# Normalized rows turned by a transposing DMA instead of TensorE: three tiles of each block's output and the third and fourth block of x

## The chip, the cores and the metric

The kernel runs on one core of a Trainium2 chip. The metric is the device time of one execution in microseconds (us). Three runs of the kernel before gave 1598.45, 1598.69 and 1598.71 us; the median is 1598.69. A core has five engines that run beside each other, each with its own queue of instructions in order: TensorE (PE; its weight loads are shown as PEld), VectorE (DVE), ScalarE (ACT), GpSimd (POOL) and SyncE (SP), which only issues transfers (DMAs) here. An instruction that waits for another engine or for a DMA holds everything behind it on its own queue.

## The reference

One transformer block on x of 2048 tokens by 512, in float32: attention of 32 heads of 16, and an MLP of width 1792, each behind a layer norm and with a residual.

```python
x = A_x
h = x + _A_ref(_layernorm(x, axis=-1), A_wqkv, A_wo)
h2 = h + _B_ref(_layernorm(h, axis=-1), B_w1, B_w2)
# _A_ref: qkv = x @ wqkv; p = softmax(q k^T * Dh**-0.5); (p v) @ wo
# _B_ref: silu(x @ w1) @ w2
```

## The kernel before

A matmul here contracts over the partitions, so normalized rows (128 tokens on the partitions, 512 features along each) have to be turned into columns (features on the partitions) before they meet a weight. For precision every operand is a pair of float16 numbers, a high part and the rest, and a product is three matmuls: high by high, rest by high, high by rest (`product`, L134). A turned tile is therefore two results: `turn` (L225) does four TensorE transposes of 128x128 with an identity (`tr`, L100, shown as L101 in the profile) into one PSUM bank, ACT copies the bank into the high part in float16 (`act`, L112), and DVE subtracts that from the bank for the rest (`low`, L123; recorded by `dve` at L115 or `pool` at L105).

Tokens go in four blocks of 512, each of four tiles of 128. The places around the change are two.

*The stage of x* (about 20 to 92 us of the span). For each block `b` the loop at L738 runs six units: two of `project_qk` (`("qk", 1)` for K, then `("qk", 0)` for Q, the columns of the first eight heads) and four of `project_v`, one for each tile. While it does so for block `b` it prepares block `b + 1`: statistics and norms (`other_ln` says in which unit), and `turn_x(b + 1, t)` (L789) for the four tiles, in units 1 to 4. Each project_qk stores its result to DRAM (`kd`, `qd`; two stores each, issued on SP), and after the second one the parts of `kd` that the first score maxima need come back, eight loads `ks<-kd` on SP (`load_k`, L778). Between and inside the units stand bursts of score maxima (`burst`, `two_max`, `maximum`): PE writes a pair of PSUM banks, DVE reduces them (`mx`, L294). In this stage blocks 1 and 2 have four PSUM banks for that, so two pairs (`lay_out(sm=range(4), ...)`, L732). ACT also issues loads of raw weights (`dma_beside`, L118) and squares them for norms.

*The output of a block* (three times, first at about 446 to 476 us). In the middle of the following block's attention, one step of the attention loop after the other, `output(b, n)` (L1172) projects tile `n` with `wo`, adds the residual, normalizes tile `n - 1` and turns it: tile 0 in step 2, tile 1 in step 3, tile 2 in step 4 and tile 3 in step 5, into `hth` and `htl`, the columns of the MLP. Right after the last of these steps `finish_block` does the values that are still due and `mlp(b)`, whose first matmul reads all four tiles. The fourth block ends in `finish_last`, with its own order of the same work.

The order on each engine is the order in which the Python code calls it (`keep_in_program_order`); nothing moves an instruction past another on its engine. A DMA also waits for the one that used its completion counter before (there are eight, given out in turn). Buffers come from pools: a tile of a pool with `bufs=2` can be written for the third time only when the readers of the first are done.

Of the kernel before, what the change touches and what calls it, by code (L numbers as in the profile page):

```python
# [10 lines left out]
F32 = mybir.dt.float32  # L11
F32R = mybir.dt.float32r
F16 = mybir.dt.float16
# [7 lines left out]
P = 128  # L21
S = 2048
D = 512
# [3 lines left out]
DC = D // P  # L27
FC = F // P
NB = S // 512
# [61 lines left out]
def attention_mlp_kernel(ctx: ExitStack, tc: tile.TileContext, x, wqkv, wo, w1, w2, out):  # L91
    nc = tc.nc
# [15 lines left out]
    def pin(ins):  # L108
        tc.keep_in_program_order(ins)

    def act(fn, *a, **k):
        pin(getattr(nc.scalar, fn)(*a, **k))  # L112
# [6 lines left out]

    def dma(*a):  # L120
        pin(nc.sync.dma_start(*a))  # L121

    def low(dst, src, high, engine="dve"):  # L123

        if high.dtype == F32R:
            high = high.bitcast(F32)
        (pool if engine == "pool" else dve)("tensor_tensor", dst, src, high, ALU.subtract)
# [22 lines left out]
    def lay_out(**rings):  # L150

        for kind, ring in rings.items():
            banks[kind] = list(ring)
# [315 lines left out]
    with ExitStack() as pa:  # L469
        pb = pa.enter_context(ExitStack())  # L470
        lay_out(sm=range(5), st=range(5, 8))
        wp = pa.enter_context(tc.tile_pool(name="wp", bufs=1))
        wvp = pb.enter_context(tc.tile_pool(name="wvp", bufs=1, side="right"))
        xp = pa.enter_context(tc.tile_pool(name="xp", bufs=3))
# [1 line left out]
        wqk_l = wp.tile([P, DC, 2 * D], F16, name="wqk_l")  # L476
        wv_h = wp.tile([P, DC, D], F16, name="wv_h")
        wv_l = wp.tile([P, DC, D], F16, name="wv_l")
        xth = [wp.tile([P, DC, 512], F16, name=f"xth{b}") for b in range(NB)]
        xtl = [wp.tile([P, DC, 512], F16, name=f"xtl{b}") for b in range(NB)]  # L480

        wqk0_h, wqk0_l = (wvp.tile([P, DC, 2 * P], F32R, name=name) for name in ("wqk0_h", "wqk0_l"))
        wv0_h, wv0_l, xth0, xtl0 = (wvp.tile([P, DC, 512], F32R, name=name) for name in ("wv0_h", "wv0_l", "xt0_h", "xt0_l"))
# [1 line left out]
        xts = [ks[2 + b % 2].rearrange("p a n -> p (a n)").bitcast(F32).rearrange("p (t d) -> p t d", d=D)  # L485
               for b in range(NB)]
# [6 lines left out]
        def load_x(b, parts=1):  # L493
            n = 4 // parts
            for t in range(0, 4, n):
                r0 = b * 512 + t * P
                dma(xts[b][:, t:t + n, :], x[r0:r0 + n * P, :].rearrange("(t p) d -> p t d", p=P))
# [11 lines left out]
        def square_rest(u):  # L509

            n = u - 7
            if 0 <= n < len(pieces):
                square_into(staged[n % 2], staged[n % 2], n)
            n = u - 5
            if 0 <= n < len(pieces):
                dma_beside(staged[n % 2], pieces[n])
# [107 lines left out]
        def project_v(b, t):  # L624
# [3 lines left out]
                  {k: (lambda n=n: burst(n)) for k, n in BESIDE_V1.get((b, t), {}).items()})  # L628
            act("mul", va[:, 4 * b + t, :, 0:DH], ps.rearrange("p (h d) -> p h d", d=DH), v_f)

        def turn_x(b, t):

            turn(xts[b][:, t, :], xth[b][:, :, t * P:(t + 1) * P], xtl[b][:, :, t * P:(t + 1) * P],
                 "sm" if b == 1 else "st")
# [10 lines left out]
        def columns(t):  # L645
            return slice(t * P, (t + 1) * P)
# [83 lines left out]
        for b in range(NB):  # L730
            if b == 1:
                lay_out(sm=range(4), st=(7, 4, 5, 6))  # L732
            if b == NB - 1:
                lay_out(sm=range(6), st=[n for n in banks["st"] if n > 5])
            units = [("qk", 1), ("qk", 0)]
            vs = [("v", t) for t in range(4)]
            found = {}
            for n, (kind, k) in enumerate(units + vs if b else units):  # L738
                tick()
                square_rest(2 + 6 * (b - 1) + n if b else n)  # L740
                rows, (stats, norm, turns) = None, ((), (), ())
                if b + 1 < NB:
                    rows = xts[b + 1]
                    stats, norm, turns = (other_ln if b else first_ln)[n]
                    if b == 2 and n < 4:
                        stats, norm = (((0, 1), (0,)), ((), (1,)), ((3,), (2,)), ((), ()))[n]

                def layer_norm():
                    for of_norm in (kind == "v", kind != "v"):
                        for t in norm if of_norm else stats:  # L750
                            if of_norm:
                                normalize(rows[:, t, :], rows[:, t, :], *found.pop(t), engine="pool" if kind == "v" and (b, n) != (1, 2) else "dve")
                            else:
                                found[t] = statistics(rows[:, t, :], LN)

                if kind == "v":
                    project_v(b, k)
                else:

                    if (b, n) == (0, 1):  # L760
                        load_x(3)
                        for c in range(2):
                            pool("tensor_scalar", scaled[1 - c], raw_v[:, 2 + c], v_w, 1.0, op0=ALU.mult, op1=ALU.mult)
                        split_qk(splits.pop((b, n)))
                    layer_norm()
                    if (b, n) == (1, 0):
                        split_values(0)
                    project_qk(b, k, scale=b > 0)
                    if (b, n) == (0, 1):
                        split_values(1)  # L770
                    if (b, n) in splits:
                        split_qk(splits.pop((b, n)))
                    if k == 0:
                        for i in range(2):
                            for h in range(4):
                                if b == 0:
                                    load_q(i, h)
                                load_k(i, h, b * 512, 512)  # L778
                if b:

                    burst(BESIDE_V[b - 1][kind == "v"][n - 2 if kind == "v" else n])
                if (b, n) == (2, 0):
                    stats, norm = (2,), ()
                if kind == "v" or (b, n) == (2, 0):
                    layer_norm()
                if (b, n) == (2, 2):
                    normalize(rows[:, 3, :], rows[:, 3, :], *found.pop(3), engine="pool")
                for t in turns:
                    turn_x(b + 1, t)  # L789
                if b == NB - 1 and n < DC:  # L790
                    split_x0(n)
                if (b, n) in splits:
                    split_qk(splits.pop((b, n)), "pool")
                if b == 2 and n in (3, 5):
                    fixed_rows(n // 4)
# [23 lines left out]
        for g in range(1, NG // 2):  # L819
            for m, (b, key) in enumerate([(b, 1) for b in range(NB)] + [(b, 0) for b in range(NB)]):  # L820
# [3 lines left out]
                n = 8 * g + m - 12  # L824
# [16 lines left out]
    cpool = ctx.enter_context(tc.tile_pool(name="cpool", bufs=1, side="right"))  # L841
    bp = ctx.enter_context(tc.tile_pool(name="bp", bufs=PTS - EARLY))
    pools.append(bp)
    gp = ctx.enter_context(tc.tile_pool(name="gp", bufs=2))
# [1 line left out]
    ot = [cpool.tile([P, 4, DC, P], F32, name=f"ot{i}") for i in range(2)]  # L846
    wo_h = cpool.tile([P, DC, D], F16, name="wo_h")
    wo_l = cpool.tile([P, DC, D], F16, name="wo_l")
    hth = cpool.tile([P, DC, 512], F16, name="hth")
    htl = cpool.tile([P, DC, 512], F16, name="htl")  # L850
    def values(g):
        i, c = divmod(g, KC)
        n = KC if i < LAST else HALF
# [118 lines left out]
    ws, hx, os = {}, {}, {}  # L972
# [8 lines left out]
    def parts_of(w):  # L981
        return w.bitcast(F16).rearrange("p (s n) -> p s n", s=2)
# [54 lines left out]
    def rows_of(b, t):  # L1037
        return ot[b % 2][:, t].rearrange("p c n -> p (c n)")

    def add_rows(b, t, ps):  # L1040

        dve("scalar_tensor_tensor", rows_of(b, t), ps, wo_f, hx[t], op0=ALU.mult, op1=ALU.add)

    def turn_rows(t):
        turn(hx.pop(t), hth[:, :, t * P:(t + 1) * P], htl[:, :, t * P:(t + 1) * P])

# [125 lines left out]
    def output(b, n):  # L1172

        if n < 4:
            ps = bank()
            weave(project_rows(n, ps), {6: lambda: singles(3)} if n < MORE[b] else {})
            add_rows(b, n, ps)
        if n == 4:

            turn_rows(n - 2)  # L1180
        if 0 < n < 5:
            normalize(hx[n - 1], rows_of(b, n - 1), *found.pop(n - 1))

        if n in (2, 3, 5):
            turn_rows(n - 2)
        if n < 4:
            found[n] = statistics(rows_of(b, n), LN)
# [144 lines left out]
    for g in range(groups):  # L1332
        tick()
        i, c = divmod(g, KC)
# [38 lines left out]
        n = maxima(g)  # L1373
# [61 lines left out]
```

## Time and profile before

| | |
|---|---|
| median of three runs | 1598.69 us |
| the profiled execution | 1598.55 us |
| its span, first to last instruction | 1596.7 us |
| PE busy | 1585.3 us (99%) |
| DVE busy | 1389.7 us (87%) |
| ACT busy | 1207.2 us (76%) |
| POOL busy | 472.6 us (30%) |
| bytes moved | 137.15 MB, mean 86 GB/s |

The profile is one execution. Each row of its timeline has the start and the length in us, the engine and line, the operation, the tile written and the tiles read, the shape and, behind an x, how many like ones were merged; a bracket names idle time of the engine just before and what ended it. Lines named for most rows are those of the recording helpers (L98 for every matmul, L112 for ACT, L115 for DVE, L105 for POOL, L121 for SP), so tiles tell the rows apart. "SPq" rows are transfers being issued by SP: their length is that of the issue, not of the transfer. A matmul's length is its way through the array (about 380 ns); those that follow each other start every 0.216 us, and that pitch is what they cost.

### The profile page before, as it was taken

Reading aid. Unit: us, or ns where it says so; the run is one execution under the profiler, and the core shown is the slowest. Engines: PE = TensorE matmul, PEld = TensorE weight load, DVE = VectorE, ACT = ScalarE, POOL = GpSimd, SP = SyncE. Lnnn points to the kernel's source line nnn. Section 1 sums busy time; section 2 is a strip of 40 time slices with the busy share of each in tenths; the row PEclk is TensorE's granted clock in tenths of the full one; section 3 lists DMA queues with packets and bytes.
Section 4 is the critical chain, followed back from the end, with each engine's and each line's share of the span. In section 5 each row is a group of like instructions: output and inputs, shape, how many; then the busy total and the mean of one; then the engine's idle time right before and its main releaser. Section 6 shows DMA issues by size and latency. Waiting matters only on the chain.

```text
span 1596.7 us, 28487 instructions
## 1 busy us (share of the span) xinstructions
PE 1585.3 (99%) x10524; PEld 477.6 (30%) x10524; DVE 1389.7 (87%) x2054; ACT 1207.2 (76%) x2384; POOL 472.6 (30%) x755
## 2 busy tenths in 40 slices
PE   9999999999999999999999999999999999999999
PEld 6434222222233322222233322222233322222254
DVE  7999999999989889999989889999987889998432
ACT  5545799999964179999963179999974189999732
POOL 5643544544426101211135101211126101211200
PEclk9999999999999999999999999999999999999999
DMA  6667533452423511121223521112133511100232
GB/s 213 173 178 221 134 86 96 107 127 81 116 67 101 156 49 35 39 54 39 50 76 100 152 53 33 39 43 51 49 77 107 159 39 37 34 12 22 74 86 73
DMA packets 111427, 137.15 MB, mean 86 GB/s; under 512 B 29136, under 2 KB 66064, under 8 KB 111288
## 3 DMA queue, kind: packets, MB, share of 16 engines
q1 hardware_dynamic: 104980, 125.17, 29.1%
q10 hardware_dynamic: 6308, 10.17, 2.3%
q8 instruction: 82, 1.34, 0.4%
q14 instruction: 57, 0.47, 0.1%
HBM read 104.68 MB, written 24.85 MB: 81 GB/s over the span
## 4 chain that ended last, share of the span: by engine, by line
PE 71%; ACT 22%; DVE 4%; DMA 1%; issue 1%; POOL 1%; SPq 0%; POOLq 0%; ACTq 0%
PE ps L98 70%; ACT pt L112 22%; DVE mx L294 2%; DVE mx L296 1%; PE ps L101 1%; DMA va<-in_A_wqkv_dram 0%; DMA ks<-in_A_x_dram 0%; DVE st L115 0%; DVE htl L115 0%; DVE hx L115 0%; SPq L121 0%; POOL rs L105 0%; POOL wv_l L105 0%; DVE xtl L115 0%; DVE ot L115 0%
## 5 line engine op out<-in xcount | busy, mean ns | idle before, releaser
L112 ACT ACTIVATE pt<-ps 128x512 f32<-128x512 f32 x2048 | 1009.4, 640 | 147.6 <-PE ps L98 145.8
L296 DVE TENSOR_REDUCE mx<-ps 128x1 f32<-128x512 f32 x1470 | 924.4, 683 | 52.3 <-PE ps L98 23.7
L98 PE MATMUL ps<-pt,va 128*17 128x512 f32 x4096 | 537.5, 598 | 0.3
L98 PE MATMUL ps<-qs,ks 64*128 64x512 f16 x2048 | 532.1, 379 | 2.3 <-DVE htl L115 0.7
L98 PE MATMUL ps<-ks,qs 48*128 48x512 f16 x2048 | 493.7, 380 | 1.5 <-DVE mx L294 1.0
L294 DVE TENSOR_REDUCE mx<-ps 128x2 f32<-128x1024 f32 x289 | 334.9, 1217 | 41.9 <-PE ps L98 40.6
L98 PEld LDWEIGHTS <-ks 64*128 64x128 f16 x2048 | 149.3, 95 | 546.0 <-issue 429.3
L105 POOL TENSOR_TENSOR ri<-rc,minus 128x16 f32<-128x16 f32 x31 | 90.7, 2925 | 235.8 <-DMA rc<-dn 169.9
L98 PE MATMUL ps<-w,gh 128*128 128x512 f16 (+1 forms) x678 | 154.4, 378 | 0.0
L98 PEld LDWEIGHTS <-qs 48*128 48x128 f16 x2048 | 126.2, 94 | 75.1 <-issue 58.3
L98 PEld LDWEIGHTS ps<-pt,va 128*17 128x17 f32 x4096 | 68.8, 95 | 223.9 <-issue 205.4
L98 PE MATMUL ps<-hth,w 128*128 128x512 f16 (+1 forms) x472 | 132.9, 369 | 0.0
L112 ACT ACTIVATE g<-ps,factors 128x512 f32<-128x512 f32 x56 | 38.5, 688 | 123.5 <-PE ps L98 95.4
L105 POOL TENSOR_TENSOR mx<-mx 128x32 f32<-128x32 f32 x52 | 12.5, 240 | 391.2 <-DVE mx L296 384.6
L98 PEld LDWEIGHTS <-w 128*128 128x128 f16 x708 | 66.3, 98 | 80.1 <-issue 12.4
L98 PEld LDWEIGHTS <-gh 128*128 128x128 f16 x678 | 63.1, 98 | 83.0 <-issue 13.7
L98 PE MATMUL ps<-htl,w 128*128 128x512 f16 (+1 forms) x236 | 84.0, 368 | 0.0
L112 ACT ACTIVATE ks<-ps 128x512 f32<-128x512 f32 x30 | 18.0, 599 | 50.3 <-PE ps L98 43.3
L115 DVE SCALAR_TENSOR_TENSOR gh<-g,factors,gh 128x512 f16<-128x512 f32 x14 | 10.5, 751 | 52.2 <-ACT gh L112 52.2
L105 POOL TENSOR_TENSOR sl<-ks,sh 128x512 f16<-128x512 f32 x30 | 34.7, 1156 | 51.5 <-ACT sh L112 34.2
L105 POOL TENSOR_TENSOR gh<-g,gh 128x512 f16<-128x512 f32 x42 | 48.5, 1155 | 3.5
L105 POOL TENSOR_TENSOR ot<-ot,den 128x512 f32<-128x512 f32 (+1 forms) x16 | 20.4, 1274 | 89.9 <-DMA den<-dr 85.5
(155 smaller groups left out, 973.8 us busy)
## 6 DMA issues: line engine op xcount, KB each, us to landing
w<-w2d SPq DMA_DIRECT2D x98, 256.0 KB
ks<-kd SPq DMA_DIRECT2D x120, 192.0 KB
w<-w1d SPq DMA_DIRECT2D x56, 256.0 KB
ks<-in_B_w_dram ACTq DMA_DIRECT2D x28, 256.0 KB
w<-in_B_w_dram SPq DMA_DIRECT2D x28, 256.0 KB
qs<-qd SPq DMA_DIRECT2D x128, 48.0 KB
kd<-sh SPq DMA_DIRECT2D x16, 256.0 KB
qd<-sh SPq DMA_DIRECT2D x16, 256.0 KB
```

Of the source, the lines that this page charges most:

```text
L98: tc.keep_in_program_order(nc.tensor.matmul(*a, **k))
L101: tc.keep_in_program_order(nc.tensor.transpose(*a))
L105: tc.keep_in_program_order(getattr(nc.gpsimd, op)(*a, **k))
L112: pin(getattr(nc.scalar, fn)(*a, **k))
L115: pin(getattr(nc.vector, fn)(*a, **k))
L294: pin(nc.vector.tensor_reduce(of, space[:, n:n + 2, :], axis=AX.X, op=ALU.max))
L296: pin(nc.vector.tensor_reduce(of[:, j:j + 1], space[:, n, :], axis=AX.X, op=ALU.max))
```

## The change

`turn_beside` is a transposing DMA on SP's queue: it takes a tile that holds, for 128 tokens, the high parts of 512 features and then the rests (128 by 1024 in float16, 256 KB) and writes it turned, as eight pieces of 128x128, into the columns of the tile pair.

For x, blocks 2 and 3 (the third and fourth; `if b:`) are no longer turned by PE. `split_x` makes high part and rest in token order out of the normalized rows, on ACT and DVE, into `xh`, a tile of a pool with two buffers; it stands ahead of the unit's projection. The DMA that turns it stands where `turn_x` stood. Block 1 is turned as before. For the output, tiles 0, 1 and 2 of the three blocks that `output` serves are split right after their norm, the high part on ACT and the rest on POOL, and turned by a DMA one step later; tile 3 is turned by PE as before. `xth` and `xtl` of a block, and `hth` and `htl`, become halves of one tile each, so that one DMA can write both.

```diff
+    def turn_beside(dst, cols, src):
+
+        pin(nc.sync.dma_start(dst.rearrange("p s c n -> p (s c) n")[:, :, cols],
+                              src.rearrange("p s d -> p (s d)"), transpose=True))
...
-        xth = [wp.tile([P, DC, 512], F16, name=f"xth{b}") for b in range(NB)]
-        xtl = [wp.tile([P, DC, 512], F16, name=f"xtl{b}") for b in range(NB)]
+        xt = [wp.tile([P, 2, DC, 512], F16, name=f"xt{b}") for b in range(NB)]
+        xth, xtl = ([t[:, r] for t in xt] for r in range(2))
...
+        def split_x(b, t):
+            h = halves[t] = xp.tile([P, 2, D], F16, name="xh", bufs=2)
+            act("copy", h[:, 0], xts[b][:, t, :])
+            low(h[:, 1], xts[b][:, t, :], h[:, 0])
...
+                if b:
+                    for t in turns:
+                        split_x(b + 1, t)
                 if kind == "v":
                     project_v(b, k)
...
                 for t in turns:
-                    turn_x(b + 1, t)
+                    if b:
+                        turn_beside(xt[b + 1], columns(t), halves.pop(t))
+                    else:
+                        turn_x(b + 1, t)
...
+    def split_normal(t):
+        rows, halves[t] = hx.pop(t), parts_of(gp.tile([P, 512], F32, name="g"))
+        act("copy", halves[t][:, 0], rows)
+        low(halves[t][:, 1], rows, halves[t][:, 0], "pool")
...
-        if n == 4:
-
-            turn_rows(n - 2)
+        if n - 2 in halves:
+            t = n - 2
+            turn_beside(hts, slice(t * P, (t + 1) * P), halves.pop(t))
         if 0 < n < 5:
             normalize(hx[n - 1], rows_of(b, n - 1), *found.pop(n - 1))
-
-        if n in (2, 3, 5):
+            if n < 4:
+                split_normal(n - 1)
+
+        if n == 5:
             turn_rows(n - 2)
```

Three places show where the new instructions stand. The first is SP's queue during block 1 of x, from the last two loads of `kd` on (a name in brackets is a counter that the instruction waits for: DMAHW0 to DMAHW7 are those of transfers, the others those of engines). Before:

```order
L121 DMA ks_101<-kd 48x512 [waits DMAHW6_49]
L121 DMA ks_101<-kd 48x512 [waits DMAHW7_49]
L121 DMA kd<-sh 128x2x512 [waits DMAHW2_49,Activation_49]
L121 DMA kd<-sl 128x512 [waits DMAHW4_49,Pool_49]
L121 DMA qd<-sh 128x2x512 [waits DMAHW5_49,Activation_49]
```

And now:

```order
L121 DMA ks_101<-kd 48x512 [waits DMAHW5_49]
L121 DMA ks_101<-kd 48x512 [waits DMAHW6_49]
L125 DMA_TRANSPOSE xt_125<-xh 128x8x128 [waits DMAHW7_49,DVE_49]
L125 DMA_TRANSPOSE xt_125<-xh 128x8x128 [waits DMAHW0_49,DVE_49]
L125 DMA_TRANSPOSE xt_125<-xh 128x8x128 [waits DMAHW1_49,DVE_49]
L125 DMA_TRANSPOSE xt_125<-xh 128x8x128 [waits DMAHW3_49,DVE_49]
L121 DMA kd<-sh 128x2x512 [waits DMAHW6_49,Activation_49]
L121 DMA kd<-sl 128x512 [waits DMAHW0_49,Pool_49]
```

All four turns of block 2 (`xt_125`) now stand behind block 1's eight loads on SP's queue, and ahead of block 2's stores.

The second is ACT in the same units: `va` is the copy that ends a unit of V, `xth` the high part out of PSUM, `xh` the new high part out of the normalized rows (`ks_103`). Before:

```order
L112 CAST xth_125<-ps 128x4x128 [waits PE_49]
L112 ACTIVATE va<-ps,v_f 128x32x16 [waits DVE_49,PE_49]
L112 CAST xth_125<-ps 128x4x128 [waits PE_49]
L112 ACTIVATE wqk_h<-va,powers 128x4x128
L118 DMA ks_107<-in_B_w_dram 128x512 [waits DMAHW6_49]
L112 ACTIVATE va<-ps,v_f 128x32x16 [waits PE_49]
L112 CAST xth_125<-ps 128x4x128 [waits DVE_49,PE_49]
```

And now:

```order
L112 CAST xh<-ks_103 128x512 [waits DVE_49]
L112 ACTIVATE va<-ps,v_f 128x32x16 [waits PE_49]
L112 ACTIVATE wqk_h<-va,powers 128x4x128
L118 DMA ks_107<-in_B_w_dram 128x512 [waits DMAHW4_49]
L112 CAST xh<-ks_103 128x512 [waits DMAHW7_49,DVE_49]
L112 ACTIVATE va<-ps,v_f 128x32x16 [waits PE_49]
```

The split of a tile now stands ahead of its unit's `va`, and that of the third tile (the last `xh` shown) waits for DMAHW7, the counter of the first transposing DMA.

The third is POOL during the output of the first block; `rs` is a tile's scale, `oh` the rest of the rows that `wo` multiplies, `g` the new rest of the normalized rows. Before:

```order
L105 TENSOR_TENSOR oh<-ot_1864,oh 128x512
L105 TENSOR_SCALAR rs<-mv 128x1
L105 TENSOR_TENSOR rs<-rs,expos 128x1
L105 TENSOR_TENSOR oh<-ot_1864,oh 128x512
L105 TENSOR_SCALAR rs<-mv 128x1
L105 TENSOR_TENSOR rs<-rs,expos 128x1
```

And now:

```order
L105 TENSOR_TENSOR oh<-ot_1844,oh 128x512
L105 TENSOR_TENSOR g<-hx,g 128x512
L105 TENSOR_SCALAR rs<-mv 128x1
L105 TENSOR_TENSOR rs<-rs,expos 128x1
L105 TENSOR_TENSOR oh<-ot_1844,oh 128x512
L105 TENSOR_TENSOR g<-hx,g 128x512
L105 TENSOR_SCALAR rs<-mv 128x1
L105 TENSOR_TENSOR rs<-rs,expos 128x1
```

The rest of a tile's normalized rows now stands ahead of the next tile's scale on POOL.

More of the change, by code (lines that the diff above doesn't have):

```diff
@@ L629, in project_v @@
             act("mul", va[:, 4 * b + t, :, 0:DH], ps.rearrange("p (h d) -> p h d", d=DH), v_f)
+        def split_x(b, t):
+            h = halves[t] = xp.tile([P, 2, D], F16, name="xh", bufs=2)
+            act("copy", h[:, 0], xts[b][:, t, :])
+            low(h[:, 1], xts[b][:, t, :], h[:, 0])
+        halves = {}
         def turn_x(b, t):
@@ L848, in attention_mlp_kernel @@
     wo_l = cpool.tile([P, DC, D], F16, name="wo_l")
-    hth = cpool.tile([P, DC, 512], F16, name="hth")
-    htl = cpool.tile([P, DC, 512], F16, name="htl")
+    hts = cpool.tile([P, 2, DC, 512], F16, name="hts")
+    hth, htl = hts[:, 0], hts[:, 1]
     def values(g):
@@ L1042, in add_rows @@
         dve("scalar_tensor_tensor", rows_of(b, t), ps, wo_f, hx[t], op0=ALU.mult, op1=ALU.add)
+    halves = {}
+    def split_normal(t):
+        rows, halves[t] = hx.pop(t), parts_of(gp.tile([P, 512], F32, name="g"))
+        act("copy", halves[t][:, 0], rows)
+        low(halves[t][:, 1], rows, halves[t][:, 0], "pool")
     def turn_rows(t):
```

## The prediction

> **What bounds the kernel now.** I read the page first (busy shares, the clock line, the chain that ended last), then the stretches of the stage of x, then the timelines of PE, SP, ACT and DVE around the turns.
>
> ```profile
> PE 1585.3 (99%) x10524; PEld 477.6 (30%) x10524; DVE 1389.7 (87%) x2054; ACT 1207.2 (76%) x2384; POOL 472.6 (30%) x755
> ...
> PEclk9999999999999999999999999999999999999999
> ...
> PE 71%; ACT 22%; DVE 4%; DMA 1%; issue 1%; POOL 1%; SPq 0%; POOLq 0%; ACTq 0%
> ```
>
> PE is idle for 11 of 1596.7 us. So a turn that leaves PE is time saved where PE runs without gaps, and any new wait of PE is added to the end, since no stage has slack in which to win it back. The timeline of PE in the stage of x, in its fourth unit of V for block 2 (the third block), has the price of a turn:
>
> ```profile
> 49.81 0.39 PE L98 MATMUL ps<-xth,wqk_h 128*128 128x512 f16 x1
> ...
> 67.21 0.66 PE L101 MATMUL ps<-ident,ks 128*128 128x128 f32 x4
> 67.70 0.38 PE L98 MATMUL ps<-wv_h,xth 128*128 128x512 f16 x1
> ...
> 70.08 0.38 PE L98 MATMUL ps<-wv_l,xth 128*128 128x512 f16 x1
> 70.39 0.60 PE L98 MATMUL ps<-ks,qs 48*128 48x512 f16 x4
> 70.92 0.39 PE L98 MATMUL ps<-xth,wqk_h 128*128 128x512 f16 x1
> ```
>
> A turn costs PE 67.70 - 67.21 = 0.49 us, a unit of V 2.69 (67.70 to 70.39, twelve matmuls at 0.216), a burst of two pairs 0.53. Block 2 begins at 49.81 and block 3 at 70.92; both moments need all four turned tiles of the new block. In the output the same rows read:
>
> ```profile
> 462.12 0.60 PE L101 MATMUL ps<-ident,hx 128*128 128x128 f32 x4
> 462.65 1.05 PE L98 MATMUL ps<-pt,va 128*17 128x512 f32 x8
> ...
> 467.30 0.60 PE L101 MATMUL ps<-ident,hx 128*128 128x128 f32 x4
> ...
> 476.40 0.60 PE L98 MATMUL ps<-hth,w 128*128 128x512 f16 x2
> ```
>
> A turn there is 0.53 us, and the MLP begins at 476.40. If nothing else changed, PE would win 8 x 0.49 + 9 x 0.53 = 8.7 us. What decides is when the transposing DMAs land.
>
> **The stage of x: when the turns are issued.** SP's queue, with issue lengths:
>
> ```profile
> 43.68 0.41 SPq L121 DMA_DIRECT2D kd<-sl  x1
> ...
> 48.01 3.57 SPq L121 DMA_DIRECT2D ks<-kd  x8
> ...
> 59.06 3.93 SPq L121 DMA_DIRECT2D ks<-kd  x8
> 63.03 0.76 SPq L121 DMA_DIRECT2D qs<-fix_q  x1
> ...
> 65.11 0.93 SPq L121 DMA_DIRECT2D ks<-fix_k  x1
> ...
> 173.19 1.77 SPq L121 DMA_DIRECT2D md<-mt  x4
> 176.01 0.53 SPq L121 DMA_DIRECT2D qs<-md  x2
> ```
>
> SP is far behind the code in block 1: it has the eight loads of `kd` out only at 48.01 + 3.57 = 51.6, when PE is already in block 2. All four turns of block 2 stand behind these loads. So the first of them is issued at 51.6 at the earliest, though its rows are ready near 35.
>
> How long a turn takes from issue to landing, L, no row shows. A store of 128 KB (`kd<-sl`, issued at 43.68) let the loads that wait for it go at 48.01: 4.3 us. A store of 2 KB (the last `md<-mt`, issued at 173.19 + 3/4 x 1.77 = 174.5) let its reader go at 176.01: 1.5 us. A turn moves 256 KB in pieces, so I take L = 4.3, the row nearest in size, with 1.5 as the lower end and two such stores one after the other, 8.6, as the upper.
>
> **The first stall.** `xh` has two buffers, so ACT's split of the third tile waits until the first turn has landed, R = 51.6 + 4.3 = 55.9. Behind it on ACT stand the `va` copies; behind its rest on DVE stand the reductions of the bursts. Their prices:
>
> ```profile
> 38.39 0.70 ACT L112 ACTIVATE va<-ps,v_f 128x512 f32<-128x512 f32 x1
> 38.98 0.59 ACT L112 CAST xth<-ps 128x512 f16<-128x512 f32 x1
> 39.30 0.39 ACTq L118 DMA_DIRECT2D ks<-in_B_w_dram  x1
> 39.44 0.74 ACT L112 ACTIVATE wqk_h<-va,powers 128x512 f16<-128x512 f32 x1
> ...
> 74.88 0.61 ACT L112 CAST xth<-xt_h 128x512 f16<-128x512 f32 x1
> ```
>
> ```profile
> 43.39 4.60 DVE L294 TENSOR_REDUCE mx<-ps 128x2 f32<-128x1024 f32 x4
> 47.91 0.67 DVE L115 TENSOR_TENSOR xtl<-ps,xth 128x512 f16<-128x512 f32 x1
> ```
>
> ```profile
> 42.30 0.39 PE L98 MATMUL ps<-ks,qs 48*128 48x512 f16 x2
> 42.92 0.39 PE L98 MATMUL ps<-ks,qs 48*128 48x512 f16 x2 [0.22 <-DVE mx L294]
> ```
>
> PE reaches the burst inside the third unit of V (42.30 before) at 42.30 - 3 x 0.49 = 40.8, finds both bank pairs full, and waits: the reduction that frees one stands on DVE behind the split of the third tile. Step by step from R: ACT's cast 0.61 and DVE's rest 0.67 end at R + 1.3, and the third turn is issued; the two reductions (47.91 - 43.39 = 4.52 for four, 1.13 each) end at R + 2.4 and 3.55, and PE writes the unit's two pairs there. The fourth tile's cast comes on ACT after one `va`, one `wqk_h` and an issue, at R + 2.2 to 2.85; its rest on DVE ends at R + 4.15, and the fourth turn is issued. Then DVE has four more reductions, to R + 8.7, before PE's last two pairs can be written; PE meanwhile does the other 8 matmuls of the unit (to R + 5.6), a burst (to R + 6.7) and the fourth unit of V (to R + 9.3). With the last burst, 0.53, block 2 begins at R + 9.85 = 65.75. The fourth turn lands at R + 4.15 + 4.3 = R + 8.45 and is not the last. Against 49.81 that is **15.9 us later**, the turns that PE no longer does already taken off.
>
> **The second stall.** Call the start of block 2 S. SP has its eight loads out 63.03 - 49.81 = 13.2 us after it, and the first turn of block 3 goes there; it lands at S + 17.5 = R2. Again the third split waits for it. PE has its third unit of V done at S + 15.1 and waits for a bank pair; DVE's rest ends at R2 + 1.3, its reductions at R2 + 2.4 and 3.55, PE has its last unit at R2 + 6.4 and the burst at R2 + 6.95. The fourth turn is later: on SP it stands behind the third (R2 + 1.3, whose issue I put at 1.0, between the 0.4 of a load and the 1.8 of four) and the four loads of fixed rows (63.03 to 66.04, 3.0), so it goes at R2 + 5.3 and lands at R2 + 9.6 = S + 27.1. Before it was 70.92 - 49.81 = 21.1: **6.0 us later**.
>
> **The array after an idle time.** The granted clock reads full throughout, also at the start, and yet:
>
> ```profile
> 1.53 4.53 PE L101 MATMUL ps<-ident 128*128 128x128 f32 x20 [1.53 <-POOL ident masks.py:199]
> ...
> 6.96 0.60 PE L101 MATMUL ps<-ident 128*128 128x128 f32 x4
> 7.40 0.62 PE L101 MATMUL ps<-ident,ks 128*128 128x128 f32 x4
> ```
>
> The first 20 transposes took 0.227 us each, four of the same a little later (7.40 - 6.96)/4 = 0.11. After idling from 40.8 to 58 PE should be as slow for its first 4 us: the 8 matmuls lose 1.7 and the bursts some tenths, of which a wait for a reduction gives 0.8 back, and the unit after them loses the rest. I put **2.0 us**; 0 to 4 are possible. After the second stall the landing covers it.
>
> The Trainium skill, "TensorE: Matmul & The Clock Gate", Part 1, says that the array falls to half its clock after an idle window of about 3.4 us and needs as long to recover. By that, an estimate from its figures, each of the two stalls would cost 1.7, together 3.4 in place of 2.0, and the time would be 1.4 us longer. The start of this trace agrees with it in kind.
>
> **The output.** Removed are three turns of 0.53 in each of three blocks. The moved work: ACT's casts replace as many; the rests go from DVE to POOL.
>
> ```profile
> 461.53 1.16 POOL L105 TENSOR_TENSOR oh<-ot,oh 128x512 f16<-128x512 f32 x1 [0.95 <-ACT oh L112]
> ```
>
> ```profile
> 467.56 0.75 DVE L115 SCALAR_TENSOR_TENSOR ot<-ps,factors,hx 128x512 f32<-128x512 f32 x1 [0.79 <-issue]
> 468.22 0.54 DVE L115 TENSOR_SCALAR hx<-ot,mv,rs 128x512 f32<-128x512 f32 x1
> ```
>
> The last turn decides. Its rows are normalized by 468.76 before; one turn less ahead of them, 468.2. ACT's cast ends at 468.8 and POOL's rest, 1.16, at 470.05; SP waits for nothing else there. With 4.3 it lands at 474.35. The MLP, three turns earlier, would begin at 476.40 - 1.6 = 474.8. So it is just hidden, by 0.45 us; from L = 4.75 on the MLP waits, and from L = 6.35 on the gain is gone. The exponentials behind the casts on ACT move by about 0.6 us, which the two steps after cover. POOL's scales come 1.2 later, still ahead of their norms. Gain: 3 x 1.6 = **4.8 us**.
>
> **Sum.** 15.9 + 6.0 + 2.0 - 4.8 = +19.1 on the profiled execution's 1598.55 us (1596.7 span and 1.85 around it): 1617.7. The median of the runs is 0.14 above that execution: 1617.8 us.
>
> **Rivals.** *Faster, since the turns are issued in time.* If SP sent the first turn before 36, it would have landed when ACT comes to the third split (after `wqk_h`, 40.2) and no queue would stop. Then the 8.7 us are won: 1590.0. For it: the rows are ready near 35, and the DMA engines have room. Against it: SP's loads end at 51.6, and the turns stand behind them. It decides at about 15 us less on SP. I give 0.06.
>
> *No change*, within 0.2% (3.2 us, about what a measurement of this kernel can tell from none): the x stage loses about 5 us and the output wins them back. That needs the first turn landed by about 45. 0.04.
>
> *The turns are slow.* With L = 8.6 block 2 waits for its fourth turn: 51.6 + 8.6 + 4.15 + 8.6 = 72.95, 23.1 later; block 3 for its own: 13.2 + 8.6 + 5.3 + 8.6 - 21.1 = 14.6 later; the last turn of an output lands at 478.65, so each of three MLPs begins 2.25 later than before, 6.8; with up to 4 for the slow array, +48: about 1647. For it: every element of 256 KB changes its partition, which no transfer here does. Against it: the traffic is twice that of the row only, and SP's queue is otherwise short. 0.10.
>
> The Trainium skill speaks for this rival: "VectorE: DVE Perf Modes", section "The three transpose paths", gives 1309 ns for a 128x128 turn by DMA against 390 on TensorE. Eight pieces in a row would be 10.5 us, an estimate from that page, beyond my upper end; no run here shows it yet.
>
> **Numbers.** Forecast 0.80 (L of 1.5 to about 6.5), the rivals 0.10, 0.06 and 0.04. At L = 1.5, without a slow array: 13.1 + 0.6 - 4.8 = +8.9, 1607.6; the stores ahead of the loads may also land earlier with ACT's own loads held back, so I go to 1605. At L = 6.5: 18.9 + 10.4 + 2 + 0.5 = +31.8, 1630; with 4 for the array 1633. The range 1605 to 1633 leaves out the three rivals, 0.20. Slower 0.90, same 0.04, faster 0.06.
>
> **What would show it.** After: a gap of PE from about 41 to 58 and a second of some us in block 3's preparation; ACT's `xh` rows waiting for a DMA; the turns on SP from 51.6 on; block 2 beginning near 66 and block 3 near 93; three output stretches shorter by 1.6 us with no wait of the first MLP matmul for `hts`. Wrong it is if SP issues the turns before 45, if L lies beyond 1.5 to 8.6, or if the output gives less than 1 us a block.

## The result, and the profile after

The changed kernel took 1617.37 us (median of four runs, 1616.65 to 1619.24) against 1598.57 us of the kernel before on the same chip (four runs, 1598.00 to 1598.71): a ratio of 1.0119, 95% interval 1.0107 to 1.0132. It is 18.8 us slower; 1617.8 was forecast. The profiled execution is the slowest of the four (1619.24 us, span 1617.3), so its span lies 20.6 us above the 1596.7 of before, 1.8 more than the medians do; the accounts below are of that execution.

From the page of the changed kernel: busy time, the granted clock in 40 slices, and the chain that ended last.

```profile
PE 1582.4 (98%) x10456; PEld 471.4 (29%) x10456; DVE 1387.8 (86%) x2045; ACT 1205.9 (75%) x2384; POOL 484.8 (30%) x764
...
PEclk9799999999999999999999999999999999999999
...
PE 81%; ACT 7%; DVE 5%; DMA 2%; issue 2%; POOL 1%; SPq 1%; POOLq 0%; ACTq 0%; DVEq 0%
```

PE has 68 transposes fewer and still only 2.9 us less busy time: it was slow for a while. The second slice, 40 to 81 us, is the only one in which the clock is below nine tenths, and that is the stage of x.

SP's queue there (the length is that of the issue; in a row of several it takes in the waits between them, as in the 9.06 us of the four turns):

```profile
45.31 3.58 SPq L121 DMA_DIRECT2D ks<-kd  x8
48.99 9.06 SPq L125 DMA_TRANSPOSE xt<-xh  x4
...
74.22 3.63 SPq L121 DMA_DIRECT2D ks<-kd  x8
77.95 7.18 SPq L125 DMA_TRANSPOSE xt<-xh  x3
85.17 0.78 SPq L121 DMA_DIRECT2D qs<-fix_q  x1
...
88.12 1.66 SPq L125 DMA_TRANSPOSE xt<-xh  x1
```

The turns of block 2 go out from 48.99, behind the eight loads of `kd`; the fourth of block 3 goes out at 88.12, behind the fixed rows. What waits for them on ACT, with what ended the wait in the bracket:

```profile
52.41 0.62 ACT L112 CAST xh<-ks 128x512 f16<-128x512 f32 x1 [12.16 <-DMA xt<-xh]
...
81.54 0.62 ACT L112 CAST xh<-ks 128x512 f16<-128x512 f32 x1 [5.93 <-DMA xt<-xh]
```

On DVE, the rest of the third tile and the reductions behind it, and the rest of the third tile in the second stall:

```profile
53.06 0.69 DVE L115 TENSOR_TENSOR xh<-ks,xh 128x512 f16<-128x512 f32 x1 [11.98 <-ACT xh L112]
53.66 2.35 DVE L299 TENSOR_REDUCE mx<-ps 128x2 f32<-128x1024 f32 x2
...
82.19 1.67 DVE L115 TENSOR_TENSOR xh<-ks,xh 128x512 f16<-128x512 f32 x1 [4.01 <-ACT xh L112]
```

On PE, the burst that waits, the starts of block 2 and block 3, and the second stall:

```profile
54.94 0.61 PE L98 MATMUL ps<-ks,qs 48*128 48x512 f16 x2 [13.24 <-DVE mx L299]
...
64.65 0.39 PE L98 MATMUL ps<-xt,wqk_h 128*128 128x512 f16 x1
...
85.05 0.39 PE L98 MATMUL ps<-ks,qs 48*128 48x512 f16 x2 [4.18 <-DVE mx L299]
...
92.75 0.38 PE L98 MATMUL ps<-xt,wqk_h 128*128 128x512 f16 x1 [1.58 <-DMA xt<-xh]
```

The third split stands on ACT until the first turn has landed, its rest stands on DVE, the reductions behind it are what PE waits for. Block 2 begins at 64.65 in place of 49.81, 14.8 us later; block 3 at 92.75 in place of 70.92, 21.8 later, so the second stall adds 7.0.

PE in stretches of 1 us (busy time, matmuls, then the granted clock, the DMA share and GB/s):

```profile
44.00:45.00 1.00, 0.00 (x0) 0.85 1.04 339
45.00:46.00 1.00, 0.00 (x0) 0.50 0.89 297
...
61.00:62.00 1.00, 1.00 (x5) 0.61 0.00 0
```

PE stopped at 41.7. The clock is halved from about 44.7 on, and it comes back only near 61.8, so that PE's work from 54.94 to there goes at half pace.

In the output of the first block the turns are landed in time (no row of the MLP waits for `hts`), and yet next to nothing is won. ACT there:

```profile
480.54 0.62 ACT L112 CAST g<-hx 128x512 f16<-128x512 f32 x1 [2.94 <-DVE hx L115]
481.07 2.05 ACT L112 ACTIVATE pt<-ps 128x512 f32<-128x512 f32 x4
```

PE in the same steps, and its first matmul of the MLP:

```profile
481.71 0.59 PE L98 MATMUL ps<-wo_h,oh 128*128 128x512 f16 x2 [0.54 <-ACT pt L112]
...
486.96 0.59 PE L98 MATMUL ps<-wo_h,oh 128*128 128x512 f16 x2 [0.54 <-ACT pt L112]
...
497.79 1.47 PE L98 MATMUL ps<-hts,w 128*128 128x512 f16 x6
```

The new cast (`g<-hx`) stands ahead of four exponentials on ACT, so the PSUM bank that the next projection needs comes free later, and PE waits 0.54 us twice. Against the 21.83 us by which block 3 of x began late, the MLP begins 497.79 - 476.40 = 21.39 late: 0.4 us won in place of 1.6. Over the rest of the span it is 21.83 - 20.6 = 1.2 us in place of 4.8.

### The profile page after: what moved, and what is told of

Read it like the earlier page. It is cut to its first block, busy times and chain, and to the rows that moved or that the text cites. A ratio compares the mean times of both kernels' runs of the same rounds, so it can differ in the third digit from the quotient of the medians.

```text
span 1617.3 us, 28404 instructions
## 1 busy us (share of the span) xinstructions
PE 1582.4 (98%) x10456; PEld 471.4 (29%) x10456; DVE 1387.8 (86%) x2045; ACT 1205.9 (75%) x2384; POOL 484.8 (30%) x764
## 4 chain that ended last, share of the span: by engine, by line
PE 81%; ACT 7%; DVE 5%; DMA 2%; issue 2%; POOL 1%; SPq 1%; POOLq 0%; ACTq 0%; DVEq 0%
PE ps L98 81%; ACT pt L112 7%; DVE mx L299 2%; DVE mx L301 1%; DMA xt<-xh 1%; SPq L121 1%; POOL g L105 1%; POOL rs L105 1%; DVE hx L115 0%; DVE pvs L115 0%; PE ps L101 0%; DMA va<-in_A_wqkv_dram 0%; ACT g L112 0%; DMA ks<-in_A_x_dram 0%; DVE st L115 0%
## 5 line engine op out<-in xcount | busy, mean ns | idle before, releaser
L98 PE MATMUL ps<-hts,w 128*128 128x512 f16 (+1 forms) x708 | 153.8, 369 | 0.0
L98 PEld LDWEIGHTS <-w 128*128 128x128 f16 x708 | 66.3, 98 | 80.1 <-issue 12.4
L98 PE MATMUL ps<-xt,wqk_h 128*128 128x512 f16 x240 | 76.0, 380 | 1.6 <-DMA xt<-xh 1.6
L115 DVE SCALAR_TENSOR_TENSOR gh<-g,factors,gh 128x512 f16<-128x512 f32 x14 | 10.5, 751 | 52.1 <-ACT gh L112 52.1
```

The source lines that it names most:

```text
L98: tc.keep_in_program_order(nc.tensor.matmul(*a, **k))
L115: pin(getattr(nc.vector, fn)(*a, **k))
```

## Experiments

Each ratio is to the kernel before on the same chip, which took 1598.45 us beside the first four kernels, 1598.34 beside the next four and 1598.60 beside the last two.

### Each half alone

Output alone: x is turned by PE as before.

```diff
-                if b:
+                if False:
                     for t in turns:
                         split_x(b + 1, t)
...
-                    if b:
+                    if False:
                         turn_beside(xt[b + 1], columns(t), halves.pop(t))
```

> Only the output's three tiles per block are turned by DMA; x is turned by TensorE as in the kernel before. Theory now (the casts on ACT put off the exponentials, so PE gets back only 0.3 us a block): 1598.6 - 0.8 = 1597.8 us. As first predicted (1.6 us a block won): 1593.8 us. Rival, that the turns land too late for the MLP: above 1598.6 us.

It took 1597.45 us, ratio 0.9993 (0.9984 to 1.0003). The forecast gain of 4.8 us isn't there; the 1.0 us that is left can't be told from none.

x alone: `output` as in the kernel before.

```diff
-        if n - 2 in halves:
-            t = n - 2
-            turn_beside(hts, slice(t * P, (t + 1) * P), halves.pop(t))
+        if n == 4:
+            turn_rows(n - 2)
...
-            if n < 4:
-                split_normal(n - 1)
...
-        if n == 5:
+        if n in (2, 3, 5):
             turn_rows(n - 2)
```

> Only x of blocks 2 and 3 is turned by DMA; the output is as in the kernel before. Theory (all of the loss lies in the stage of x): 1617.4 + 0.8 = 1618.2 us. As first predicted, with 4.8 us won in the output: 1617.4 + 4.8 = 1622.2 us. Rival, that the output costs a part of the loss: below 1617 us.

It took 1619.76 us, ratio 1.0129 (1.0114 to 1.0145): 21.3 us slower. All of the loss is in the stage of x, and the two halves add up (21.3 - 1.0 = 20.3; together they were measured at 18.8, with about 2 us of uncertainty on each).

### Is the ring of two what stops the queues?

```diff
-            h = halves[t] = xp.tile([P, 2, D], F16, name="xh", bufs=2)
+            h = halves[t] = xp.tile([P, 2, D], F16, name="xh", bufs=4)
```

> The changed kernel with four buffers for xh in place of two, nothing else. Theory (the ring of two lets ACT and DVE stop behind the first turn): the four turns go out one after the other from 49.0 us at 1.3 us each, the last lands near 56.3, block 2 begins there and not at 64.65 (8.3 us earlier); block 3 some 4.6 us earlier, since its fourth turn still stands behind the loads of fixed rows: 1617.4 - 12.9 = 1604.5 us. Rival, that SP's order alone holds PE: the turns leave no earlier and it stays within 2 us of 1617.4. Rival, that the transfers themselves are slow: likewise 1615 to 1618 us.

It took 1618.50 us, ratio 1.0127 (1.0111 to 1.0142). The theory that the ring is the cause fell. SP in this kernel:

```profile
49.66 6.16 SPq L125 DMA_TRANSPOSE xt<-xh  x4
...
81.63 1.64 SPq L125 DMA_TRANSPOSE xt<-xh  x1
```

And PE:

```profile
58.87 0.58 PE L98 MATMUL ps<-xt,wqk_h 128*128 128x512 f16 x1 [4.98 <-DMA xt<-xh]
...
89.33 0.58 PE L98 MATMUL ps<-xt,wqk_h 128*128 128x512 f16 x1 [7.43 <-DMA xt<-xh]
```

ACT and DVE no longer stop for a landing, but the turns go out no earlier than with two, one behind the other for 6.16 us, and PE waits for the fourth itself. Block 2 begins 5.8 us earlier than in the changed kernel, but its first twelve matmuls now run at half pace (5.2 us, to 64.08, in place of 2.7), and block 3's fourth turn, issued at 81.63, lands 7.7 us later. With SP's order as it is, the ring only decides which engine shows the wait. Whether a ring of two would matter with the loads out of the way on SP was not run.

### Is turning slow?

The same bytes by a plain DMA; the kernel leaves out the turning.

```diff
-                              src.rearrange("p s d -> p (s d)"), transpose=True))
+                              src.rearrange("p s (c n) -> p (s c) n", n=P)))
```

> The changed kernel with each transposing DMA replaced by a plain DMA of the same bytes, from the same place on SP's queue to the same tiles (so the columns aren't turned, and the output is not the reference's). Theory (place in the queue and ring, not the turning): the issue is some 0.9 us shorter and the landing perhaps 1 us, so 3 to 5 us less, 1612 to 1615 us. Rival, that turning is what is slow: most of the loss goes, 1596 to 1602 us.

It took 1619.26 us, ratio 1.0128 (1.0113 to 1.0144). SP in this kernel:

```profile
49.10 8.22 SPq L125 DMA_DIRECT2D xt<-xh  x4
```

And ACT:

```profile
52.32 0.62 ACT L112 CAST xh<-ks 128x512 f16<-128x512 f32 x1 [12.57 <-DMA xt<-xh]
```

The plain copy lands 52.32 - 49.10 = 3.2 us after its issue, the turn 52.41 - 48.99 = 3.4. So the transposing costs next to nothing in the landing. It costs issue time: block 3's fourth transfer held SP for 0.66 us as a copy and for 1.66 as a turn. Neither expectation (a gain of several us from the plain copy) came true.

### The turns ahead of the loads on SP

Four buffers, and the loads of `kd` of blocks 1 and 2 behind the turns.

```diff
-                                load_k(i, h, b * 512, 512)
+                                if b in (0, NB - 1):
+                                    load_k(i, h, b * 512, 512)
...
+                if 0 < b < NB - 1 and n == 4:
+                    for i in range(2):
+                        for h in range(4):
+                            load_k(i, h, b * 512, 512)
```

> Four buffers of xh, and the eight loads of kd of block 1 and of block 2 issued behind the four turns on SP; the turns themselves as they are. Theory (the turns are late because of what SP has ahead of them): SP is done with block 1's stores at about 43.7, the four turns follow at 1.5 us each, the last at 48.3, and lands 3.5 to 4 us later; block 2 begins near 52.5 in place of 58.9 with four buffers alone, without the half pace. Block 3's fourth turn still stands behind the fixed rows, but nothing else; together 1603 to 1609 us. Rival (a turn takes 7 to 9 us from issue to landing whatever is ahead of it when four follow each other): block 2 begins at 56 or later, and the time stays at 1613 or above.

It took 1608.21 us, ratio 1.0057 (1.0042 to 1.0073), within the 1603 to 1609 expected. Half of the loss is gone: four buffers alone gave nothing, so the order on SP was needed for it. The order without the two more buffers was not run. SP here:

```profile
44.47 5.64 SPq L125 DMA_TRANSPOSE xt<-xh  x4
...
72.65 1.64 SPq L125 DMA_TRANSPOSE xt<-xh  x1
```

And PE:

```profile
44.27 0.61 PE L98 MATMUL ps<-ks,qs 48*128 48x512 f16 x2 [3.07 <-DVE mx L299]
...
53.89 0.39 PE L98 MATMUL ps<-xt,wqk_h 128*128 128x512 f16 x1
...
79.60 0.58 PE L98 MATMUL ps<-xt,wqk_h 128*128 128x512 f16 x1 [4.62 <-DMA xt<-xh]
```

Block 2 no longer waits for a transfer and still begins 4.1 us late (53.89, where 52.5 without half pace was expected). Here a second cause comes to light, which the long stall had covered. DVE in this kernel:

```profile
38.75 0.69 DVE L115 TENSOR_TENSOR xh<-ks,xh 128x512 f16<-128x512 f32 x1 [0.80 <-ACT xh L112]
...
41.42 1.66 DVE L115 TENSOR_TENSOR xh<-ks,xh 128x512 f16<-128x512 f32 x1 [0.68 <-ACT xh L112]
43.00 2.34 DVE L299 TENSOR_REDUCE mx<-ps 128x2 f32<-128x1024 f32 x2
```

POOL at the same time:

```profile
41.38 1.15 POOL L105 TENSOR_TENSOR wqk_l<-va,wqk_h 128x512 f16<-128x512 f32 x1
```

The rest of a split reads two tiles in SBUF. Begun 0.04 us behind POOL's instruction it took 1.66 us in place of 0.69; the rest of the kernel before reads PSUM and takes 0.66 to 0.69 in this stage. With the waits for ACT's cast the first reduction runs at 43.00, 2.5 us later than the 40.53 of before, and PE waits 3.07 us for it, after which the clock is halved again. That stall needs no slow transfer at all. In block 3 the fourth turn still stands behind the fixed rows and lands 79.60 - 72.65 = 7.0 us after its issue.

### The turns on ACT's queue

With two buffers, and then with four.

```diff
-    def turn_beside(dst, cols, src):
-
-        pin(nc.sync.dma_start(dst.rearrange("p s c n -> p (s c) n")[:, :, cols],
+    def turn_beside(dst, cols, src, queue=nc.sync):
+
+        pin(queue.dma_start(dst.rearrange("p s c n -> p (s c) n")[:, :, cols],
...
-                        turn_beside(xt[b + 1], columns(t), halves.pop(t))
+                        turn_beside(xt[b + 1], columns(t), halves.pop(t), nc.scalar)
```

> The four turns of blocks 2 and 3 issued on ACT's queue in place of SP's, two buffers of xh as in the changed kernel. Theory (SP's place in the queue is the cause, the ring only shows it): the turns go out at about 38.5, 42, 45 and 48 and land 3.5 us later; block 2 begins at 51 to 53, block 3 21 to 24 us behind it; 1597 to 1604 us. Rival (the ring of two is the cause wherever the turns are issued, since the third split must wait for a landing): a wait of ACT of 5 us or more for the third split stays, and the time is 1609 or above. Rival (an issue of 1.3 to 1.7 us holds ACT, whose copies PE waits for): waits of PE for ACT of some us in the stage of x, 1605 to 1610.

> Four buffers of xh and the turns on ACT's queue. Theory: no split waits, the fourth turn of block 2 goes out by 47 and lands by 50.5, that of block 3 is not behind the fixed rows; 1595 to 1600 us, 1 to 4 less than with two buffers on ACT. If the landing itself is what is slow (7 us, as the fourth turn of block 3 was with four buffers on SP), block 2 begins near 54 and the time is 1602 or above.

They took 1607.47 us (ratio 1.0058, 1.0043 to 1.0074) and 1609.67 us (1.0064, 1.0049 to 1.0079). Both forecasts of my theory were missed, by 3 and by 10 us; the rival that an issue holds ACT came true in its time and its cause, at both sizes of the ring, but what PE waits for is DVE behind ACT, not ACT. With two buffers the third split no longer waits for a landing, so the ring alone is not the cause either. Block 2 begins at 54.51 with four buffers, as the other rival had it, but not for a late landing: all that waits for a turn there is a weight load of PE, by 0.5 us. ACT with four buffers:

```profile
40.72 1.26 ACTq L125 DMA_TRANSPOSE xt<-xh  x1
...
42.67 0.62 ACT L112 CAST xh<-ks 128x512 f16<-128x512 f32 x1
```

DVE's rest of the third tile:

```profile
43.32 0.77 DVE L115 TENSOR_TENSOR xh<-ks,xh 128x512 f16<-128x512 f32 x1 [2.17 <-ACT xh L112]
```

And PE's burst behind it:

```profile
45.27 0.61 PE L98 MATMUL ps<-ks,qs 48*128 48x512 f16 x2 [4.14 <-DVE mx L299]
```

The turn waits on ACT for DVE's rest and then takes 1.26 us to issue; the next cast stands behind it, the next rest behind the cast, the reductions behind the rest. Where SP's queue was the obstacle, ACT's has become one, at half the price.

### The output with its cast on DVE

x as before, and the high part of the normalized rows on DVE.

```diff
-        act("copy", halves[t][:, 0], rows)
+        dve("tensor_copy", halves[t][:, 0], rows)
```

> The output's part alone (x turned by PE as before), with the high part of the normalized rows cast on DVE in place of ACT. Theory (ACT's cast stands ahead of the exponentials, and PE loses there what the removed turns give): the exponentials come 0.5 to 0.6 earlier in two or three steps of each block, a gain of 0.8 to 1.4 us a block on top of 0.3; 1593.5 to 1596 us. Rival (DVE, 87% busy, becomes the wait in ACT's place): 1597 us or above, and PE waits for the maxima or for ot by about as much as it did for ACT.

It took 1595.00 us, ratio 0.9979 (0.9970 to 0.9988), and 1595.20 (0.9978, 0.9969 to 0.9987) in the repetition. All waits of PE for the exponentials between 60 and 1590 us, as totals, in the kernel with the output alone (the changed kernel has the same row); with the cast on DVE no such row is left:

```profile
PE ps L98 <- ACT pt L112: 3.2, 6, 0.5
```

The cast on DVE, in the first of the two runs:

```profile
458.52 0.43 DVE L115 CAST g<-hx 128x512 f16<-128x512 f32 x1
```

And PE's first matmul of the first MLP in the same run:

```profile
474.87 1.47 PE L98 MATMUL ps<-hts,w 128*128 128x512 f16 x6
```

The MLP begins 476.40 - 474.87 = 1.53 us earlier than before, nearly the 1.6 that three removed transposes were to give. The cast costs DVE 0.43 us, and PE waits for DVE no more than before (0.8 us between 60 and 1590, where it was 2.0).

> The output's part alone with its cast on DVE once more, beside the kernel with block 3 added: 1594.4 to 1595.6 us.

### Block 3 alone, with nothing ahead of its turns

On top of the last kernel, beside its repetition: block 3 of x turned by DMA with four buffers, block 2 by PE; block 2's loads of `kd` and all loads of fixed rows behind the four turns.

```diff
-                                load_k(i, h, b * 512, 512)
+                                if b != 2:
+                                    load_k(i, h, b * 512, 512)
...
+                if (b, n) == (2, 4):
+                    fixed_rows(0)
+                    for i in range(2):
+                        for h in range(4):
+                            load_k(i, h, b * 512, 512)
...
-                if b == 2 and n in (3, 5):
+                if b == 2 and n == 5:
                     fixed_rows(n // 4)
```

> On top of the output's part with its cast on DVE (1595.0 us): block 3 of x alone turned by transposing DMAs, block 2 by PE as before; four buffers, and on SP the four turns stand ahead of block 2's eight loads of kd and of all loads of fixed rows. Theory (a turn is hidden where nothing stands ahead of it): the turns go out from 13 to 22 us after block 2 began, the last lands by 25 at most with 3.5 us each, PE does not wait for it; and PE wins at most 4 x 0.49 = 2.0 us there, less what DVE, busy 4.9 of 5 us in these units, does not give. 1593.0 to 1595.5 us, block 3 beginning 19 to 21.1 us after block 2. Rival (a fourth turn takes 7 us to land whatever stands ahead of it): PE waits for it by 3 us or more, 1597 or above.

It took 1595.08 us, ratio 0.9979 (0.9970 to 0.9988), the same as the 1595.20 of the kernel without block 3. SP's fourth turn:

```profile
67.72 1.24 SPq L125 DMA_TRANSPOSE xt<-xh  x1
```

On ACT the cast that this turn waits for, and on DVE the rest:

```profile
66.35 0.62 ACT L112 CAST xh<-ks 128x512 f16<-128x512 f32 x1 [2.69 <-POOL ks L105]
```

```profile
67.00 0.69 DVE L115 TENSOR_TENSOR xh<-ks,xh 128x512 f16<-128x512 f32 x1 [1.30 <-ACT xh L112]
```

And PE, from the start of block 2 to that of block 3:

```profile
49.34 0.39 PE L98 MATMUL ps<-xt,wqk_h 128*128 128x512 f16 x1
...
59.23 0.39 PE L98 MATMUL ps<-ks,qs 48*128 48x512 f16 x2 [0.55 <-DVE mx L299]
...
70.01 0.39 PE L98 MATMUL ps<-ks,qs 48*128 48x512 f16 x2 [0.74 <-DVE mx L299]
71.06 0.38 PE L98 MATMUL ps<-xt,wqk_h 128*128 128x512 f16 x1 [0.66 <-DMA xt<-xh]
```

Two things follow. With the fixed rows behind it the fourth turn lands 71.06 - 67.72 = 3.3 us after its issue; behind them it took 7.0 and 7.7 with four buffers, though only 4.6 in the changed kernel, so how much they cost a turn is not settled. And PE wins nothing: block 3 begins 21.7 us after block 2, with four transposes fewer, where it was 21.1 before (19 to 21.1 were expected). Its waits of 0.55, 0.74 and 0.66 us take 1.95, all that four transposes of 0.49 were to give. The first is for a DVE without a gap. A stretch of the kernel before (busy time and count of PE, PEld, DVE, ACT and POOL, clock, DMA share, GB/s):

```profile
56.00:61.00 5.00, 5.00 (x30) 2.53 (x29) 4.93 (x8) 3.52 (x8) 4.13 (x4) 1.00 0.62 188
```

The same stretch in this kernel:

```profile
56.00:61.00 5.00, 4.45 (x22) 1.79 (x21) 5.00 (x7) 4.16 (x10) 4.43 (x4) 1.00 0.81 206
```

DVE was as full as PE there. The other two waits have another cause by the trace: POOL has normalized the fourth tile's rows only at 66.3, so ACT's cast and DVE's rest come late, DVE stands still for 1.30 us with reductions behind that rest, and the turn lands 0.66 us too late for PE, which was expected not to wait for it. The best version of the study is the output's part alone with the cast on DVE: 1595.0 us, 3.3 us faster than the kernel before.

## Why the prediction was right, and where it was not

The time was right, 1617.8 against 1617.37, and that it came so close is luck, by errors that cancel: on the profiled execution the stage of x cost 21.8 us where 23.9 were forecast, and the output gave 1.2 where 4.8 were. That leaves 1.5 us too few, and the median lies 1.9 below that execution. What carries the forecast is the mechanism of the two stalls.

*The first stall.* The mechanism was right step by step: the turns behind the eight loads of `kd` on SP, ACT's third split waiting for the first landing, DVE behind ACT, PE behind DVE for a gap of 13.2 us. The two sizes that it starts from were too long. The first turn went out at 48.99, not 51.6, since the loads ahead of it started at 45.31 and not 48.01, although the store that they wait for (43.09) was hardly earlier. The prediction had named a reason and not priced it, ACT's own loads held back, and the traces fit it: in the three kernels where ACT stops ahead of its second load of raw weights (the changed one, x alone, the plain copy) the loads start 2.2 us after that store's issue, and in the others with the loads in that place 3.8 to 5.4 us after it. No run varies this alone. The landing took 3.4 us, not 4.3; the row that 4.3 was taken from was thus no good measure of a transfer. From the landing on, the chain of nine steps was forecast to take 9.85 us, or 11.85 with the slow array; it took 64.65 - 52.41 = 12.24. So the start of block 2 was 1.1 us earlier than the forecast without the slow array, 3.1 with it.

*The rests of the split* were priced at 0.67 us by a row that reads PSUM. That term was mis-sized: behind an instruction of POOL they take up to 1.67, in the changed kernel too. It cost nothing in the first stall (0.69 for the third tile). In the second stall the third tile's rest took 1.67, and the third turn, the fixed rows and the fourth turn stand behind it on SP: 1.0 us. With the loads moved it is part of the 3.07 us that PE waits. The Trainium skill, "SBUF — State Buffer", section "SBUF: two separate sides", says that DVE and GpSimd share a pair of ports under an exclusive lock, also for a DVE instruction with two SBUF inputs; the 1.66 us beside POOL's 1.15 agree with it.

*The ring* was named together with SP's order as one cause. The run with four buffers separates them: without the ring's wait the time is the same.

*The second stall* was 7.0 us, 6.0 were forecast. The path was as told, down to the fourth turn behind the fixed rows; it was issued 23.5 us after block 2 began (22.8 forecast) and landed 4.6 us later (4.3). The first landing came 0.6 us earlier than forecast, the third tile's rest took 1.0 longer.

*The slow array* was put at 2.0 us for the first stall, and is 2.4 by the chain above. It is the clock: the granted clock falls to 0.50 at 44.7, 3.0 us after PE stops, and in the second stall at 85.7, 4.8 us after PE stops and 0.6 after it has begun again. After the second stall block 3 waits for its turn anyway, as told. The Trainium skill, "TensorE: Matmul & The Clock Gate", Part 1, gives about 3.4 us of idling for the fall and about as much work for the recovery. The trace agrees with the length, as a step (the last section has it): the recovery took two such steps of work after the first stall, 54.94 to 61.8, and one after the second, 85.7 to 89.1.

*The output* is the step that failed, by the prediction's own sign (less than 1 us a block): "The exponentials behind the casts on ACT move by about 0.6 us, which the two steps after cover." Nothing covers them, since the next projection needs the bank that they free: PE waits 0.54 us in six places, 3.2 in all. The last tile's rows come later too, their scale being behind POOL's rest: PE waits 1.2 us for them in place of 0.8. That is the missing 3.6. With the cast on DVE the waits for the exponentials are gone, the first block gives 1.53 us, and the output as a whole 3.3 to 3.4 in place of 1.0. In the two profiled executions with that cast the third MLP begins 4.2 and 4.0 us earlier than before, near the 4.8; the last block loses 0.8 and 0.2 of it again, in the first of them 0.7 by a wait of PE for `qs<-mn`, which the other doesn't have.

*The rivals.* "The turns are slow" is excluded by the 3.4 us and by the plain copy. From the Trainium skill, "VectorE: DVE Perf Modes", section "The three transpose paths" (1309 ns for one piece), came an estimate of 10.5 us for eight pieces in a row; the trace doesn't agree, eight pieces landed in 3.4. "Faster, since the turns are issued in time" was rightly made unlikely, but its price of 8.7 us was too high: of the 3.9 us in the stage of x nothing was won where it was tried, on block 3 (not on block 2), where 0.55 us went to a full DVE (4.9 of 5 us busy before) and 1.40 to rows that are normalized too late for the longer way through cast, rest and transfer. The prediction had read PE alone as the bound of that stage.

## What to carry to other kernels

Before a transfer replaces work of a busy engine, look up what stands ahead of it on the issuing queue at the moment when its data are ready, including loads that themselves wait; a deeper ring or another queue moved the wait here, because neither queue was free. When work goes to an engine with time to spare, ask which buffer the work behind it frees and who needs that next: 0.6 us of idle-looking ACT cost PE the whole gain, and the same cast on DVE cost nothing. And before counting a saving on the busiest engine, check in that stage's stretches whether a second engine is just as full, and whether the data are ready early enough for the longer way.

## What the runs showed of the hardware beyond what was expected

The granted clock changes on a grid. In the changed kernel it falls at 44.71, returns at 61.77, falls at 85.66 and returns at 89.08: 17.06, 23.89 and 3.42 us apart, which is 5, 7 and 1 steps of 3.41. In the six other kernels of this study whose clock fell in the stage of x, all changes there lie whole steps of 3.41 us apart as well. By these runs it is how busy PE was within one step that counts, so a wait of 2.2 us can halve the clock after work has begun again. With four buffers and the turns on ACT, PE waited 2.16 us for block 3 and began at 80.57 at full pace. The step in which that falls, and the next:

```profile
78.00:81.41 3.41, 1.23 (x6) 1.00 1.15 188
81.41:84.82 3.41, 3.41 (x9) 0.50 0.33 87
```

With two buffers the same wait was 1.64 us, and the clock stayed full; the step in which it lies, counted on from that run's own changes:

```profile
78.07:81.49 3.42, 1.65 (x8) 1.00 0.98 181
```

In those seven kernels, from 24 to 95 us, each step at full clock in which PE was busy for at most 0.36 of it was followed by half the clock, and none with 0.48 or more was. How busy a step must be for the clock to return is less clear: one of 0.78 was enough, one of 0.85 was not.

An issue of a transposing DMA of 256 KB held SP for 1.23 to 2.28 us in the changed kernel and ACT for 1.25 to 1.43, where a load of `kd` takes 0.45 (3.58 us for eight). Four in a row are therefore some 6 us of a queue, more than the 3.4 us that one of them takes to land.
